# The last two chunks' down-projection of five feature pairs with seven block products for eight, columns by tokens

## The chip, the cores and the metric

The kernel runs on one core of a Trainium2 chip. The metric is the device time of one execution in microseconds (us). The core has five engines that run beside each other and wait for each other by semaphores: TensorE (PE, with its weight loads listed as PEld), VectorE (DVE), ScalarE (ACT), GpSimd (POOL) and SyncE (SP, which here only issues transfers). Matmuls read SBUF and write banks of PSUM (eight banks of 128 x 512 floats); DVE and ACT read and write both memories, POOL only SBUF.

## The reference

Strided attention on 8 x 8 heads gives 4608 tokens of 512 features, and two matrices follow, with the square of a ReLU between them:

```python
x = attn_out.transpose(0, 2, 1, 3).reshape(B * S, H * D)   # 4608 x 512
h = np.maximum(x @ w_in, 0.0)                              # w_in 512 x 2048
return (h * h @ w_out).astype(np.float32)                  # w_out 2048 x 512
```

Called here the up-projection (`x @ w_in`) and the down-projection (`h * h @ w_out`), in float32.

## The kernel before

**Precision.** A float32 matrix is kept as two fp32r tiles, high part and remainder, and each product is three matmuls: high by high, low by high, high by low. To split an operand, ACT casts the high part and another engine subtracts it (`features`, L720 and L721: ACT, then DVE).

**Tiling.** The tokens are nine chunks of 512 (`TC`), the 2048 features sixteen tiles of 128 (`NFT`), in eight pairs `p` of two (features 2p and 2p+1). `wi[p]` and `wo[p]` hold a pair's weights, as high and low. The up-projection (`up`, L738) gives a feature tile as 128 features x 512 tokens in one bank; ACT applies ReLU and square (`squared`, L725 and L726). The down-projection (`downs`, L772) uses 128 tokens of the squared tile as stationary operand and 512 columns of `w_out` as moving one: four banks of 128 tokens x 512 columns (`y_ps`) add up over the sixteen features, twelve matmuls a feature.

**The last two chunks.** Call them a (chunk 7) and b (chunk 8). Their pairs 0 to 2 (`MIX` = 3) go as above, and both chunks' up-projections of pairs 3 to 7 go together in `finale`, as 2 x 2 blocks by Winograd's form of Strassen's scheme: seven products (`product`, L994, six matmuls each) for eight. It needs differences of weights, made per pair by `combos` (L972 to L987 on POOL, ten instructions of 128 x 256, then L967 on ACT and L968 on DVE, four times each), and differences of the chunks' activations (`ts`, made once). Between the seven products of a pair, four groups of six matmuls of chunk a's down-projection of the pair before fill PE's queue (`fill`). Then come chunk a's last two features, and last, with nothing of other engines left to do but copying out, the whole of b's down-projection: 16 features, 192 matmuls. The last two features of a and of b are ordered by bank, so that banks are copied and stored while PE goes on.

**Order.** Each engine executes its queue in order. PE's order is that of the program (`pe` puts each group behind the one before, by `tc.issue_after`). On DVE, ACT and POOL a planner that schedules on simulated times takes what is ready, earlier program lines first. A tile of a pool waits until the buffer that it takes over is free, and the first tiles of a pool that is opened where another was closed wait for the last use of that other. Stores are issued on SP's queue, and the very last half bank on ACT's.

Of the kernel before, what the change touches and what calls it, by code (L numbers as in the profile page):

```python
# [83 lines left out]
def attn_moe(ctx: ExitStack, tc, qk_d, v_d, qk_p, v_p, kv_s, q_s, k_s, v_s, w_in, w_out, masks, consts, out):  # L84
# [674 lines left out]

    def downs(c, js):  # L760
# [21 lines left out]
        if end:  # L782
            for t in range(NTT):
                y = ypool.tile([P, DM], F32, name=f"ysb{c}_{t}", tag="ysb")
                dst = out[c * TC + t * P : c * TC + (t + 1) * P, :]
                if tail and t == NTT - 1:
                    m = DM // 2
                    for i, queue in ((0, nc.sync), (m, nc.scalar)):
                        nc.scalar.copy(y[:, i : i + m], y_ps[c][t][:, i : i + m])
                        queue.dma_start(out=dst[:, i : i + m], in_=y[:, i : i + m])  # L790
                else:
                    (nc.scalar.copy if t % 2 else nc.vector.tensor_copy)(y, y_ps[c][t])
                    nc.sync.dma_start(out=dst, in_=y)
            yield done
# [120 lines left out]

    def second(p):
# [4 lines left out]
        g = home(p)  # L921
        for i in range(2):
            features(b, 2 * p + i, held[b, 2 * p + i], (g[:, i, 0], g[:, i, 1]))

    def differences():
# [3 lines left out]
        late = pool("late", 1)  # L929
# [22 lines left out]
    def finale():  # L952
# [48 lines left out]
        second(MIX - 1)  # L1001
        turn = [0, 1, 4]
        for p in range(MIX, NFT // 2):
            fill = downs(a, [2 * p - 2, 2 * p - 1])
# [10 lines left out]
            squared(ba)  # L1015
            features(a, 2 * p, ba)
            last_one = p == NFT // 2 - 1
            for _ in range(1 if last_one else 2):
                pe(lambda: next(fill))
# [4 lines left out]
            squared(c22)  # L1024
            for _ in range(1 if last_one else 2):
                pe(lambda: next(fill))
            s_next = combos(p + 1) if p + 1 < NFT // 2 else None
# [6 lines left out]
            squared(bb)
            squared(u2)
            features(a, 2 * p + 1, u2)
            g = home(p)
            for i, src in enumerate((bb, c22)):
                features(b, 2 * p + i, src, (g[:, i, 0], g[:, i, 1]))
            s = s_next  # L1040
        pe(lambda: down(a, [NFT - 2, NFT - 1]))
        for j in range(0, NFT, 2):
            pe(lambda: down(b, [j, j + 1]))
# [105 lines left out]
```

## Time and profile before

| | before |
|---|---|
| median of 3 runs (lowest to highest) | 836.65 us (836.48 to 837.39) |
| profiled execution, its own time | 836.61 us |
| its span, first to last instruction | 834.6 us |
| PE busy | 825.1 us, 99% |
| DVE, POOL, ACT busy | 552.6, 578.2, 344.9 us |
| matmuls | 5973 |

The span is what lies between the first and the last instruction that the profiler saw; 2.0 us of the profiled execution's time lie around it. A row of the timeline gives start, duration, engine, line, operation and the tiles (out<-in) with their shape, and in brackets the idle time ahead of it and what ended that. Matmuls overlap in their records (each lasts 390 ns, and the next starts earlier), so the pace is read from start to start.

### The profile page before, as it was taken

The page shows a single profiled execution, that of the slowest core. Times are in us where ns is not written, and L with a number is a line of the kernel's source. Part 1 is how long each engine was busy: PE and PEld are TensorE (multiplying, and loading weights), DVE is VectorE, ACT ScalarE, POOL GpSimd, SP SyncE. Part 2 cuts the span into 40 slices and gives each one's busy share as a digit, 9 for nine tenths or more (in the row PEclk, how much of TensorE's full clock was granted, in tenths as well). Part 3 has the DMA queues.
Part 4 walks back from the last instruction along what each step waited for, and adds up shares of the span by engine and source line. Part 5 has one row for each costly group of instructions (what it writes and reads, how often), then busy time and mean ns, then how long its engine had stood idle before and what let it go on. Part 6 is the DMA issues. An engine that isn't in the chain of part 4 may idle for free.

```text
span 834.6 us, 14916 instructions
## 1 busy us (share of the span) xinstructions
PE 825.1 (99%) x5973; PEld 677.4 (81%) x5977; DVE 552.6 (66%) x997; ACT 344.9 (41%) x610; POOL 578.2 (69%) x594
## 2 busy tenths in 40 slices
PE   8999999999999999999999999999999999999998
PEld 5788888888888888888888888888888877888886
DVE  6979866785778567775688477866887884444200
ACT  5987743333333234333333333323333256556300
POOL 4597779786996878786978599697879387640000
PEclk9999999999999999999999999999999999999999
DMA  9974350113310431042113130033023000000101
GB/s 354 394 258 138 123 200 34 58 61 122 107 57 3 153 132 59 1 156 102 39 59 119 44 130 26 13 124 118 0 80 108 28 25 0 1 1 1 50 1 51
DMA packets 23653, 73.68 MB, mean 88 GB/s; under 512 B 2592, under 2 KB 6048, under 8 KB 21920
## 3 DMA queue, kind: packets, MB, share of 16 engines
q1 hardware_dynamic: 23296, 72.49, 24.9%
q8 instruction: 47, 0.77, 0.4%
q10 hardware_dynamic: 288, 0.24, 0.1%
q14 instruction: 22, 0.18, 0.1%
HBM read 63.28 MB, written 9.44 MB: 87 GB/s over the span
## 4 chain that ended last, share of the span: by engine, by line
PE 82%; DVE 6%; POOL 6%; issue 2%; DMA 2%; ACT 2%; SPq 0%; DVEq 0%; POOLq 0%
PE y L772 40%; PE h L738 33%; PE c L994 6%; POOL pp L545 3%; PE o L296 2%; POOL pq L545 2%; DVE pt L248 1%; DMA v<-v_d 1%; PE s L281 1%; DVE os L546 1%; DVE gl L721 1%; DVE b L940 1%; ACT h L725 0%; DVE b L937 0%; ACT gh L720 0%
## 5 line engine op out<-in xcount | busy, mean ns | idle before, releaser
L772 PE MATMUL y<-w,gh 128*128 128x512 f32 x1024 | 314.6, 390 | 0.0
L545 POOL TENSOR_TENSOR pq<-ks,qs 128x512 f32<-128x512 f32 (+7 forms) x184 | 208.4, 1160 | 49.5 <-DVE sc L546 45.3
L545 POOL TENSOR_TENSOR pp<-vs,sc 128x320 f32<-128x320 f32 (+11 forms) x184 | 201.1, 1121 | 53.8 <-DVE os L546 51.2
L772 PEld LDWEIGHTS y<-w,gh 128*128 128x128 f32 x1024 | 191.7, 188 | 40.1 <-POOL w L166 0.3
L772 PE MATMUL y<-w,gl 128*128 128x512 f32 x512 | 197.8, 389 | 0.0
L725 ACT ACTIVATE h<-h 128x512 f32<-128x512 f32 x120 | 69.9, 583 | 271.9 <-PE h L738 270.9
L546 DVE TENSOR_REDUCE sc<-pq 128x5 f32<-128x320 f32 (+6 forms) x192 | 113.0, 598 | 48.1 <-POOL pq L545 46.4
L546 DVE TENSOR_REDUCE os<-pp 128x32 f32<-128x384 f32 (+15 forms) x184 | 108.8, 602 | 51.2 <-POOL pp L545 49.8
L738 PE MATMUL h<-xlh,w 128*128 128x512 f32 x496 | 135.0, 393 | 1.5 <-DVE gb L721 1.4
L738 PE MATMUL h<-xsh,w 128*128 128x512 f32 x496 | 133.1, 389 | 0.0
L721 DVE TENSOR_TENSOR gl<-h,gh 128x512 fp32r<-128x512 f32 x118 | 80.5, 683 | 64.0 <-ACT gh L720 63.8
L772 PEld LDWEIGHTS y<-w,gl 128*128 128x128 f32 x512 | 96.1, 188 | 20.0
L738 PEld LDWEIGHTS h<-xlh,w 128*128 128x128 f32 x496 | 91.9, 188 | 22.3 <-DVE gb L721 2.7
L738 PEld LDWEIGHTS h<-xsh,w 128*128 128x128 f32 x496 | 93.1, 188 | 19.5
L738 PE MATMUL h<-xll,w 128*128 128x512 f32 x248 | 76.8, 390 | 0.0
L738 PE MATMUL h<-xsl,w 128*128 128x512 f32 x248 | 76.8, 389 | 0.0
L726 ACT ACTIVATE h<-h 128x512 f32<-128x512 f32 x120 | 69.9, 582 | 3.5
L720 ACT CAST gh<-h 128x512 fp32r<-128x512 f32 x118 | 69.4, 588 | 4.1 <-DVE h L749 0.9
L166 POOL TENSOR_TENSOR w<-raw,w 128x512 fp32r<-128x512 f32 x32 | 45.6, 1430 | 19.5 <-DVE w L162 10.5
L248 DVE STREAM_TRANSPOSE pt<-e 32x256 f32<-32x256 f32 x128 | 55.7, 435 | 2.3
L738 PEld LDWEIGHTS h<-xsl,w 128*128 128x128 f32 x248 | 46.5, 188 | 9.9 <-DVE xsl L502 0.2
L738 PEld LDWEIGHTS h<-xll,w 128*128 128x128 f32 x248 | 46.5, 188 | 9.8
(164 smaller groups left out, 784.9 us busy)
## 6 DMA issues: line engine op xcount, KB each, us to landing
vs<-v_s SPq DMA_DIRECT2D x18, 576.0 KB, 3.7
v<-v_d SPq DMA_DIRECT2D x18, 512.0 KB, 4.9
y<-ysb SPq DMA_DIRECT2D x35, 256.0 KB, 2.7
raw<-w_out SPq DMA_DIRECT2D x7, 1024.0 KB, 6.3
raw<-w_in SPq DMA_DIRECT2D x6, 1024.0 KB, 7.2
ks<-k_s SPq DMA_DIRECT2D x8, 576.0 KB, 3.8
qk<-qk_d SPq DMA_DIRECT2D x8, 560.0 KB, 4.8
qk<-qk_d SPq DMA_DIRECT2D x8, 544.0 KB, 5.0
```

Of the source, the lines that this page charges most:

```text
L166: last["g"] = nc.gpsimd.tensor_sub(lo, f32(w), f32(hi))
L248: nc.vector.transpose(out=pt[to : to + STR, :, STR * b : STR * (b + 1)], in_=e5[STR * b : STR * (b + 1), :, a, STR * half : STR * (half + 1)],
L296: last["mm"] = nc.tensor.matmul(o[a][D * h : D * (h + 1), at : at + STR], v5[pr][ks, h, w, b], pt[ks, (2 * h + pr) * 2 + w, STR * b : STR ...
L545: nc.gpsimd.tensor_mul(pv, x, y)
L546: nc.vector.tensor_reduce(out=to, in_=pv, op=ALU.add, axis=AX.X)
L720: last["gh"] = nc.scalar.copy(gh, ph)
L721: last["gl"] = lows[c, j] = nc.vector.tensor_sub(gl, ph, f32(gh))
L725: nc.scalar.activation(ph, ph, AF.Relu)
L726: nc.scalar.activation(ph, ph, AF.Square)
L738: done = nc.tensor.matmul(ph, wi[p][a][:, wsl], x["ls"[k // 2], b][:, k % 2, :], start=n == 0, stop=n == 11)
L772: done = nc.tensor.matmul(y_ps[c][t], gg[:, sl], w[:, wsl], start=j == 0 and k == 0, stop=j == NFT - 1 and k == 2)
L994: done = nc.tensor.matmul(bank, w[m][:, k], x[n][:, k], start=start and k == m == n == 0, stop=True, skip_group_check=True)
```

## The change

Pairs 3 to 7 of the down-projection of a and b get the same seven-for-eight scheme. The output is turned: stationary operand 128 columns of `w_out`, moving operand 512 tokens, so that a bank holds 128 columns x 512 tokens (`turned_down`, also for all features of chunk a and for b's pairs 0 to 2), and the host swaps the axes back in `unpack`. The blocks are two halves of the 512 columns, the pair's two features, and the two chunks; one product of one pair is six matmuls, three into each of two banks (`block`).

In the loop over pairs the four groups of filling matmuls a pair become one (`fill_first`, the product of the plain blocks, of the pair before), and the squared activations are kept whole in `gf` tiles, three of the four after a subtraction. After the loop pool `late` is closed and pool `tail` opened; then PE runs `fill_first` of pair 7, b's direct products into `W`, and six products one after another, each over all five pairs (`t3`, `b21`, `t2`, `t1`, `t4`, `b22`), and last b's direct products into `Y`. Each of the six needs its moving operand split for each pair (`operand`: ACT cast, DVE subtraction, 128 x 512), `t2` and `t4` also a subtraction ahead of that, and `t3`, `t2`, `t1` and `b22` sums of weights (`third`, `firsts`, `fourth`, of 128 x 256, on POOL or DVE).

The lines that the new loop replaces stand in the kernel above.

```diff
@@ -753,6 +753,13 @@
         features(c, j, ph)
         yield done
+    def turned_down(bank, p, o, t, g, start):
+        at = slice(o * DM + t * P, o * DM + (t + 1) * P)
+        for k, (m, n) in enumerate(((0, 0), (1, 0), (0, 1))):
+            done = nc.tensor.matmul(bank, wo[p][m][:, at], g[n], start=start and k == 0, stop=True, skip_group_check=True)
+        return done
     def down(c, js):
         *_, done = downs(c, js)
         return done
@@ -763,18 +770,16 @@
             y_ps[c] = [ybank(f"y{c}_{t}") for t in range(NTT)]
         g = [g_tiles.pop((c, j)) for j in js]
         end = js[-1] == NFT - 1
-        tail = end and c == NCHUNK - 1
         def part(t, j, gh, gl):
             p, o = divmod(j, 2)
             wsl, sl = slice(o * DM, (o + 1) * DM), slice(t * P, (t + 1) * P)
+            if c == NCHUNK - 2:
+                return turned_down(y_ps[c][t], p, o, t, (gh, gl), j == 0)
             for k, (gg, w) in enumerate(((gh, wo[p][0]), (gh, wo[p][1]), (gl, wo[p][0]))):
                 done = nc.tensor.matmul(y_ps[c][t], gg[:, sl], w[:, wsl], start=j == 0 and k == 0, stop=j == NFT - 1 and k == 2)
             return done
         steps = [(t, n) for n in range(len(js)) for t in range(NTT)]
-        if end and c >= NCHUNK - 2:
-            steps.sort()
         for m, (t, n) in enumerate(steps):
             done = part(t, js[n], *g[n])
             if m % 2:
@@ -783,14 +788,8 @@
...
-                if tail and t == NTT - 1:
-                    m = DM // 2
-                    for i, queue in ((0, nc.sync), (m, nc.scalar)):
-                        nc.scalar.copy(y[:, i : i + m], y_ps[c][t][:, i : i + m])
-                        queue.dma_start(out=dst[:, i : i + m], in_=y[:, i : i + m])
-                else:
...
+                (nc.scalar.copy if t % 2 else nc.vector.tensor_copy)(y, y_ps[c][t])
+                nc.sync.dma_start(out=dst, in_=y)
...
+    of_late = ctx.enter_context(ExitStack())
...
-        late = pool("late", 1)
+        late = of_late.enter_context(tc.tile_pool(name="late", bufs=1))
...
@@ -999,48 +1002,212 @@
         with tc.issue_after(last["sum"].ins):
             s = combos(MIX)
         second(MIX - 1)
+        NP = NFT // 2
+        g, fs = {}, {}
+        def up_sums(p):
+            fs[p] = combos(p)
+        fs[MIX] = s
+        direct_fill = downs(a, [2 * MIX - 2, 2 * MIX - 1])
+        def take_direct(n):
+            for _ in range(n):
+                pe(lambda: next(direct_fill))
+        def first_product(p, bank):
+            pe(lambda: product(bank, direct(p, 0, 0), x11, True))
+        def split_to(hi, lo, src, sub=nc.vector):
+            nc.scalar.copy(hi, src)
+            sub.tensor_sub(lo, src, f32(hi))
+        def block(banks, w, op, start, ts=range(2)):
+            for t in ts:
+                for k, (m, n) in enumerate(((0, 0), (1, 0), (0, 1))):
+                    done = nc.tensor.matmul(banks[t], w[m][:, t * P : (t + 1) * P], op[n], start=start and k == 0, stop=True, skip_group_check=True)
+            return done
+        def w_block(p, o, m):
+            return [t[:, o * DM + m * 256 : o * DM + (m + 1) * 256] for t in wo[p]]
+        b11 = {}
+        def fill_first(p):
+            pe(lambda: block(X, w_block(p, 0, 0), b11[p], p == MIX))
         turn = [0, 1, 4]
...
+        ba = psum(turn[0], f"c11_{MIX}")
+        first_product(MIX, ba)
+        for p in range(MIX, NP):
             na, nb, spare = turn
             turn = [spare, na, nb]
...
+            last_one = p == NP - 1
+            bb, bc = psum(nb, f"c12_{p}"), psum(3, f"c21_{p}")
+            nc.scalar.copy(bb, ba)
+            s = fs.pop(p)
+            if p > MIX:
+                fill_first(p - 1)
             pe(lambda: product(bc, s[3], ts[3], True))
...
             pe(lambda: product(bb, s[2], ts[2], False))
             u2 = ypool.tile([P, TC], F32, name=f"u2_{p}", tag="ysb")
             nc.scalar.copy(u2, bb)
...
+            pe(lambda: product(ba, direct(p, 1, 0), x21, False))
+            if p == MIX:
+                take_direct(2)
             pe(lambda: product(bb, s[1], ts[1], False))
             c22 = ypool.tile([P, TC], F32, name=f"c22_{p}", tag="ysb")
             nc.vector.tensor_copy(c22, bb)
+            squared(ba)
+            b11[p] = [gpool.tile([P, TC], F32R, name=f"b11{t}_{p}", tag=f"g{t}") for t in "hl"]
+            split_to(*b11[p], ba)
+            if p == MIX:
+                take_direct(2)
+                ds = [gpool.tile([P, TC], F32, name=f"d{t}", tag=("gh", "gl")[t % 2]) for t in range(4)]
+                for t in range(4):
+                    (nc.vector.tensor_copy if t % 2 else nc.scalar.copy)(ds[t], y_ps[a][t])
+                X, W = ([ybank(f"{nm}{t}") for t in range(2)] for nm in "xw")
             nc.vector.tensor_add(c22, c22, bc)
...
+            if not last_one:
+                ba_next = psum(spare, f"c11_{p + 1}")
+                first_product(p + 1, ba_next)
+                up_sums(p + 1)
+            else:
+                pe(lambda: [turned_down(W[t], 0, 0, 2 + t, [gb[0][:, 0, k] for k in range(2)], True) for t in range(2)][-1])
             pe(lambda: product(bb, s[4], x22, False))
             pe(lambda: product(bc, direct(p, 1, 1), ts[4], False))
...
             nc.vector.tensor_add(u2, u2, bc)
...
+            h = g[p] = wpool.tile([P, 4, TC], F32, name=f"gf{p}", tag=f"w{HOME[order.index((p, 0))]}")
+            for i, src in ((1, bb), (3, c22), (2, u2)):
+                nc.scalar.activation(src, src, AF.Relu)
+                nc.scalar.activation(h[:, i], src, AF.Square)
+                if i == 1:
+                    nc.vector.tensor_sub(h[:, 0], h[:, 1], ba)
+            nc.vector.tensor_sub(h[:, 1], h[:, 3], h[:, 1])
+            if not last_one:
+                ba = ba_next
+        of_late.close()
+        tail = of_late.enter_context(tc.tile_pool(name="tail", bufs=1))
+        PS = range(MIX, NP)
+        sums = {n: {} for n in (1, 2, 3, 4)}
+        def part(nm, p):
+            return tail.tile([P, 256], F32, name=f"q{nm}_{p}", tag="sf", bufs=3)
+        def kept_sum(n, p, src, e):
+            t = sums[n][p] = tail.tile([P, 2, 256], F32R, name=f"v{n}_{p}", tag="sd", bufs=8)
+            nc.scalar.copy(t[:, 0], src)
+            e.tensor_sub(t[:, 1], src, f32(t[:, 0]))
+            return [t[:, 0], t[:, 1]]
+        low = {}
+        blocks = lambda p: {(m, o): [f32(t) for t in w_block(p, o, m)] for m in range(2) for o in range(2)}
+        def third(p, e):
+            w = blocks(p)
+            s3, u = part("3", p), part("u", p)
+            e.tensor_sub(s3, w[0, 0][0], w[1, 0][0])
+            e.tensor_sub(u, w[0, 0][1], w[1, 0][1])
+            e.tensor_add(s3, s3, u)
+            sums[3][p] = kept_sum(3, p, s3, e)
+        s2s = {}
+        def firsts(p, e):
+            w = blocks(p)
+            s1, u = part("1", p), part("w", p)
+            e.tensor_add(s1, w[1, 0][0], w[1, 1][0])
+            e.tensor_add(u, w[1, 0][1], w[1, 1][1])
+            e.tensor_add(s1, s1, u)
+            s2 = s2s[p] = tail.tile([P, 256], F32, name=f"q2_{p}", tag="s2", bufs=5)
+            e.tensor_sub(s2, s1, w[0, 0][0])
+            e.tensor_sub(s2, s2, w[0, 0][1])
+            sums[2][p] = kept_sum(2, p, s2, e)
+            to = sums[1][p] = w_block(p, 0, 1)
+            nc.scalar.copy(to[0], s1)
+            e.tensor_sub(to[1], s1, f32(to[0]))
+        def fourth(p, e):
+            w, s4 = blocks(p), part("4", p)
+            e.tensor_sub(s4, w[0, 1][0], s2s[p])
+            e.tensor_add(s4, s4, w[0, 1][1])
+            sums[4][p] = kept_sum(4, p, s4, e)
+        ops, tags = {}, ["xlh", "xll", "xsh", "xsl", None, "xlh", "xll", "xsh", "xsl", None, None, None]
+        def operand(nm, p, src, sub=nc.vector):
+            tag = tags.pop(0)
+            tags.append(tag)
+            t = ops[nm, p] = (xpool.tile([P, 2, TC], F32R, name=f"{nm}_{p}", tag=tag) if tag else tail.tile([P, 2, TC], F32R, name=f"{nm}_{p}", tag="op", bufs=4))
+            split_to(t[:, 0], t[:, 1], src, sub)
+        def product_of(banks, nm, w, start=False):
+            for p in PS:
+                pe(lambda: block(banks, w(p), [ops[nm, p][:, k] for k in range(2)], start and p == MIX))
+        def outs(t, m, y, queue=nc.sync):
+            r = (a + m) * TC + t * P
+            queue.dma_start(out=out[r : r + P, :], in_=y)
+        fill_first(NP - 1)
+        Y = [psum(turn[0], "ya"), psum(turn[1], "yb")]
+        Z = [psum(turn[2], "za"), psum(3, "zb")]
+        for t in range(2):
+            nc.scalar.copy(Y[t], X[t])
+        for j in range(1, 2 * MIX):
+            pe(lambda: [turned_down(W[t], *divmod(j, 2), 2 + t, g_tiles[b, j], False) for t in range(2)][-1])
+        for p in PS:
+            third(p, nc.vector if p - MIX > 2 else nc.gpsimd)
+            operand("t3", p, g[p][:, 1])
+        product_of(Z, "t3", lambda p: sums[3][p], True)
+        for p in PS:
+            operand("b21", p, g[p][:, 2])
+        product_of(X, "b21", lambda p: w_block(p, 1, 0))
+        c22 = [gpool.tile([P, TC], F32, name=f"c22{t}", tag=f"g{'hl'[t]}") for t in range(2)]
+        for t in range(2):
+            nc.scalar.copy(c22[t], W[t])
+            nc.vector.tensor_add(c22[t], c22[t], Z[t])
+        for t in range(2):
+            y = ypool.tile([P, TC], F32, name=f"y11_{t}", tag="ysb")
+            nc.vector.tensor_add(y, ds[t], X[t])
+            outs(t, 0, y)
+        for p in PS:
+            firsts(p, nc.gpsimd if (p - MIX) % 2 else nc.vector)
+            nc.vector.tensor_sub(g[p][:, 1], g[p][:, 3], g[p][:, 0])
+            operand("t2", p, g[p][:, 1])
+        product_of(Y, "t2", lambda p: sums[2][p])
+        for t in range(2):
+            nc.vector.tensor_add(ds[2 + t], ds[2 + t], Y[t])
+        for p in PS:
+            operand("t1", p, g[p][:, 0])
+            fourth(p, nc.gpsimd)
+        product_of(Y, "t1", lambda p: sums[1][p])
+        for t in range(2):
+            nc.vector.tensor_add(c22[t], c22[t], Y[t])
+            outs(2 + t, 1, c22[t])
+        for p in PS:
+            nc.vector.tensor_sub(g[p][:, 2], g[p][:, 2], g[p][:, 1])
+            operand("t4", p, g[p][:, 2])
+        product_of(Z, "t4", lambda p: w_block(p, 1, 1))
+        for t in range(2):
+            nc.vector.tensor_add(ds[2 + t], ds[2 + t], Z[t])
+            outs(2 + t, 0, ds[2 + t])
+        for p in PS:
+            operand("b22", p, g[p][:, 3])
+        product_of(Y, "b22", lambda p: sums[4][p])
+        for t in range(2):
+            for j in range(2 * MIX):
+                pe(lambda: turned_down(Y[t], *divmod(j, 2), t, g_tiles[b, j], False))
+            y = ypool.tile([P, TC], F32, name=f"y12_{t}", tag="ysb")
+            if t == 0:
+                nc.vector.tensor_copy(y, Y[t])
+                outs(t, 1, y)
+            else:
+                m = TC // 2
+                for i, queue in ((0, nc.sync), (m, nc.scalar)):
+                    nc.scalar.copy(y[:, i : i + m], Y[t][:, i : i + m])
+                    queue.dma_start(out=out[b * TC + P : b * TC + 2 * P, i : i + m], in_=y[:, i : i + m])
...
@@ -1125,6 +1292,8 @@
...
+    y = y.reshape(NCHUNK, TC, DM).copy()
+    y[-2:] = y[-2:].swapaxes(1, 2)
...
```

## Rows read from the trace of the kernel before

**Rows 1.** The page: span, and busy time of each engine

```profile
span 834.6 us, 14916 instructions
PE 825.1 (99%) x5973; PEld 677.4 (81%) x5977; DVE 552.6 (66%) x997; ACT 344.9 (41%) x610; POOL 578.2 (69%) x594
```

**Rows 2.** The chain that ended last, in order of time: start, duration, engine, line

```profile
719.04 8.16 PE c L994 x36
734.00 8.16 PE c L994 x36
...
787.17 43.87 PE y L772 x192
...
831.07 0.65 ACT ysb L789 x2
```

**Rows 3.** Stretches: length, busy time (count) of PE, PEld, DVE, ACT, POOL; granted clock; DMA

```profile
0.00:5.00 5.00, 3.19 (x93) 1.51 (x94) 0.27 (x1) 1.49 (x2) 3.00 (x7) 1.00 0.61 197
...
680.00:700.00 20.00, 18.75 (x81) 14.54 (x79) 15.40 (x18) 11.81 (x25) 18.90 (x21) 1.00 0.00 0
...
740.00:760.00 20.00, 20.00 (x90) 16.57 (x89) 9.27 (x15) 12.13 (x24) 4.75 (x6) 1.00 0.01 1
...
800.00:820.00 20.00, 20.00 (x90) 16.53 (x90) 0.00 (x0) 0.00 (x0) 0.00 (x0) 1.00 0.00 0
```

**Rows 4.** Timeline of DVE, both operands in SBUF (at 717.29 one in PSUM)

```profile
675.26 0.69 DVE L949 TENSOR_TENSOR t1l<-b,t1h 128x512 fp32r<-128x512 f32 x1
675.87 0.69 DVE L940 TENSOR_TENSOR b<-b,b 128x512 f32<-128x512 f32 x1
...
681.73 1.22 DVE L937 TENSOR_TENSOR b<-xsh,xsl 128x512 f32<-128x512 f32 x1
682.88 2.38 DVE L940 TENSOR_TENSOR b<-b,b 128x512 f32<-128x512 f32 x2
685.17 1.22 DVE L949 TENSOR_TENSOR t1l<-b,t1h 128x512 fp32r<-128x512 f32 x1
...
692.59 1.51 DVE L968 TENSOR_TENSOR s<-f,s 128x256 fp32r<-128x256 f32 x2 [1.06 <-ACT s L967]
...
716.96 0.42 DVE L968 TENSOR_TENSOR s<-f,s 128x256 fp32r<-128x256 f32 x1
717.29 0.68 DVE L1023 TENSOR_TENSOR c<-c,c 128x512 f32<-128x512 f32 x1
```

**Rows 5.** Timeline of POOL at the same times

```profile
681.21 1.20 POOL L972 TENSOR_TENSOR f<-w 128x256 f32<-128x256 f32 x1
682.37 1.19 POOL L973 TENSOR_TENSOR fu<-w 128x256 f32<-128x256 f32 x1
...
692.90 0.92 POOL L972 TENSOR_TENSOR f<-w 128x256 f32<-128x256 f32 x1
693.78 0.92 POOL L987 TENSOR_TENSOR f<-f,w 128x256 f32<-128x256 f32 x1
...
698.57 0.74 POOL L981 TENSOR_TENSOR f<-f,w 128x256 f32<-128x256 f32 x1
699.39 0.73 POOL L982 TENSOR_TENSOR f<-f,w 128x256 f32<-128x256 f32 x1
...
721.86 0.74 POOL L973 TENSOR_TENSOR fu<-w 128x256 f32<-128x256 f32 x1 [3.67 <-DVE s L968]
...
745.18 0.73 POOL L987 TENSOR_TENSOR f<-f,w 128x256 f32<-128x256 f32 x1
```

**Rows 6.** Timeline of DVE with one operand in PSUM

```profile
722.45 1.30 DVE L721 TENSOR_TENSOR gb<-c,gb 128x512 fp32r<-128x512 f32 x2
```

**Rows 7.** Groups of ACT lines from 680 us on: busy time, mean ns

```profile
L720 ACT CAST gb<-c 128x512 fp32r<-128x512 f32 x10 | 5.5, 602 | 0.4 <-PE c L994 0.4
L967 ACT CAST s<-f 128x256 fp32r<-128x256 f32 x20 | 8.1, 410 | 13.1 <-PE c L994 9.1 <-POOL f L982 3.2 <-POOL f L987 0.8
```

**Rows 8.** Timeline of PE where the loop over pairs begins

```profile
707.86 0.73 PE L994 MATMUL c<-t3h,s 128*128 128x512 f32 x2 [0.55 <-DVE gb L721]
```

More of the change, by code (lines that the diff above doesn't have):

```diff
@@ L785, in downs @@
                 dst = out[c * TC + t * P : c * TC + (t + 1) * P, :]
-                if tail and t == NTT - 1:
-                    m = DM // 2
-                    for i, queue in ((0, nc.sync), (m, nc.scalar)):
-                        nc.scalar.copy(y[:, i : i + m], y_ps[c][t][:, i : i + m])
-                        queue.dma_start(out=dst[:, i : i + m], in_=y[:, i : i + m])
-                else:
-                    (nc.scalar.copy if t % 2 else nc.vector.tensor_copy)(y, y_ps[c][t])
-                    nc.sync.dma_start(out=dst, in_=y)
+                (nc.scalar.copy if t % 2 else nc.vector.tensor_copy)(y, y_ps[c][t])
+                nc.sync.dma_start(out=dst, in_=y)
             yield done
@@ L914, in home @@
         return wpool.tile([P, 2, 2, TC], F32R, name=f"gb{p}", tag=f"w{HOME[order.index((p, 0))]}")
+    gb = {}
     def second(p):
@@ L920, in second @@
             pe(lambda: list(up(b, j, (3, 4)[j % 2]))[-1])
-        g = home(p)
+        g = gb[p] = home(p)
         for i in range(2):
             features(b, 2 * p + i, held[b, 2 * p + i], (g[:, i, 0], g[:, i, 1]))
+    of_late = ctx.enter_context(ExitStack())
     def differences():
@@ L1001, in finale @@
         second(MIX - 1)
+        NP = NFT // 2
[22 more added lines that the diff above has]
+            pe(lambda: block(X, w_block(p, 0, 0), b11[p], p == MIX))
         turn = [0, 1, 4]
-        for p in range(MIX, NFT // 2):
-            fill = downs(a, [2 * p - 2, 2 * p - 1])
+        ba = psum(turn[0], f"c11_{MIX}")
+        first_product(MIX, ba)
+        for p in range(MIX, NP):
             na, nb, spare = turn
             turn = [spare, na, nb]
-            ba, bb, bc = psum(na, f"c11_{p}"), psum(nb, f"c12_{p}"), psum(3, f"c21_{p}")
-            pe(lambda: product(ba, direct(p, 0, 0), x11, True))
+            last_one = p == NP - 1
[4 more added lines that the diff above has]
+                fill_first(p - 1)
             pe(lambda: product(bc, s[3], ts[3], True))
-            nc.scalar.copy(bb, ba)
-            pe(lambda: product(ba, direct(p, 1, 0), x21, False))
             pe(lambda: product(bb, s[2], ts[2], False))
@@ L1014, in finale @@
             nc.scalar.copy(u2, bb)
[L1015 to L1019, printed above, removed]
+            pe(lambda: product(ba, direct(p, 1, 0), x21, False))
+            if p == MIX:
+                take_direct(2)
             pe(lambda: product(bb, s[1], ts[1], False))
@@ L1022, in finale @@
             nc.vector.tensor_copy(c22, bb)
-            nc.vector.tensor_add(c22, c22, bc)
[L1024 to L1027, printed above, removed]
+            squared(ba)
[7 more added lines that the diff above has]
+                X, W = ([ybank(f"{nm}{t}") for t in range(2)] for nm in "xw")
@@ L1028, in finale @@
+            nc.vector.tensor_add(c22, c22, bc)
+            if not last_one:
[4 more added lines that the diff above has]
+                pe(lambda: [turned_down(W[t], 0, 0, 2 + t, [gb[0][:, 0, k] for k in range(2)], True) for t in range(2)][-1])
             pe(lambda: product(bb, s[4], x22, False))
             pe(lambda: product(bc, direct(p, 1, 1), ts[4], False))
-            if last_one:
-                for _ in range(2):
-                    pe(lambda: next(fill))
@@ L1033, in finale @@
             nc.vector.tensor_add(u2, u2, bc)
[L1034 to L1043, printed above, removed]
+            h = g[p] = wpool.tile([P, 4, TC], F32, name=f"gf{p}", tag=f"w{HOME[order.index((p, 0))]}")
```

## The prediction

> **What bounds the kernel now.** The page's busy times come first: PE is busy 825.1 of 834.6 us, every other engine 70% or less [rows 1]. The chain of waits ends in PE alone: blocks of 36 matmuls in the loop over pairs, then 192 in one piece, then two half copies and the last store [rows 2]. Two pairs start 14.96 us apart (734.00 - 719.04) with 42 + 24 = 66 matmuls each: 0.2267 us a matmul, back to back. In the stretches, POOL's work is over by 746 us [rows 5] and nobody but PE works from 800 to 820 us [rows 3]. So PE's count sets the time of the finale, and the other engines have some 40 us of room at the end. The change takes from the first and fills the second.
>
> **PE's side of the sum.** Before, the finale has 5 x 42 up, 5 x 24 fillers, 24 of chunk a's last features and 192 of b: 546 matmuls. After: 5 x 42 up; seven products of 30, the fillers among them, 210; direct ones 24 (a's pair 2) + 36 (`W`) + 36 (`Y`): 516. Instructions of the same shape, so 30 x 0.2267 = 6.8 us go. The end stays: 18 matmuls into the last bank, two half copies, a store of each half; nine stores before and nine after, SP's queue has room. The wait of 0.55 us at the loop's start [rows 8] stays too, since bank 3 is written second in either order.
>
> **The loop over pairs.** A pair shrinks from 66 matmuls to 48, 14.96 to 10.88 us. ACT's 512-wide operations go from 14 to 11 a pair and DVE's from 7 to 6 (the 256-wide ones of `combos` stay); POOL's ten stay, 1.2 each where DVE is always at work [rows 5], 12 us, and 8.2 us alone. The nearest new chain: the next pair's `bb` takes the bank of this pair's `ba`, which isn't free until ACT's square (0.60, after the pair's last product since it lands in the place of `wi[p]`), DVE's subtraction of `ba` (0.69) and ACT's copy (0.60) are through, about 2.1 us with the hand-overs, against 18 matmuls, 4.1 us. That hides it. Without cover it is 4 turns x 2.1. Bounds: 0, and 4 x (14.96 - 10.88) = 16 if POOL's pauses (3.67 us in one wait for DVE [rows 5]) don't shrink with the pair. POOL's waits follow products of PE, which come closer together as well, so I take 0.5.
>
> **The six products after the loop.** Call T0 the end of the loop's last product. PE then has 36 matmuls with nothing to wait for (8.2 us), and then six products of five blocks (1.36 us each). What they need, counted from the diff: ACT 30 casts of 512 and 20 of 256, 0.60 and 0.41 [rows 7], 26 us in 49: hidden. DVE 40 subtractions of 512 with both operands in SBUF (30 `operand`, 10 of `gf` tiles), 29 of 256 (`third` of two pairs 8, `firsts` of three pairs 21), and 11 of 512 with one in PSUM. POOL 41 of 256 (`third` 12, `firsts` 14, `fourth` 15).
>
> What these cost is the point. Alone, DVE does the 512 in 0.69 and the 256 in 0.42, POOL the 256 in 0.74 [rows 4, 5]; from start to start in a queue that is 0.61 to 0.62, 0.33 to 0.35 and 0.82 [rows 4, 5]. From 681 to 687 us both have work without a pause, all operands in SBUF: each DVE instruction of 512 lasts 1.15 to 1.22 us and each POOL instruction of 256 1.18 to 1.20, one beginning where the other ends, both once in 1.15 us. They take turns. Where DVE's are of 256 (two in 1.51 at 692.59), POOL's starts are 0.88 apart (692.90, 693.78). If a DVE instruction holds up POOL in proportion to its length, the difference gives 0.27 for 256 and 0.54 for 512, and POOL's own hold is 1.15 - 0.54 = 0.61. With an operand in PSUM, two DVE instructions take 1.30 while POOL works: not held up [rows 6]. So each POOL instruction can cost DVE 0.61.
>
> Take the last block of `t2`, 120 matmuls or 27.2 us after T0. By then DVE must have done: 20 of 512 (operands of `t3`, `b21`, `t2` and one row of subtractions), less four of `t3` that can run ahead of T0, 16 x 0.62 = 9.9; 29 of 256, 10.2; seven others of the loop's end and of the first sums' copying out, 7 x 0.66 = 4.6. Together 24.7 us: alone it just fits. POOL must have done 12 + 14 = 26, holding 26 x 0.61 = 15.9. If every hold falls on a waiting DVE instruction, DVE is through at 40.6, and PE has stood 13.4 us. If the two share without any loss, 15.9 + 16 x 0.54 + 29 x 0.27 = 32.4 us, begun 1.4 us ahead of T0 (pool `tail` waits for the last use of `late`, the product before the last): 31.0, PE stands 3.9. The rows of 681 to 687 show every hold landing on DVE, so I go near the upper end, less what the seven PSUM operations hide (4.6 us long, of which I take half): 11.0. The three scratch tiles (`sf`, two held by each `third` and `firsts`) push the same way. After `t2`, 90 matmuls (20.4 us) to the last block of `b22`, DVE has 20 x 0.62 + 6 x 0.66 = 16.4 and POOL holds 15 x 0.61 = 9.2: 25.6 with every hold, 9.2 + 20 x 0.54 = 20.0 shared; between 5.2 late and on time. Here `fourth` has two products' time to be made ahead, so I take 0, and leave 5.2 to the range. A wait of PE holds up everything behind it, as its order is fixed: no direct product stands between the six.
>
> **Sum**, against the profiled execution's 836.6 (median 836.65): - 6.8 + 0.5 + 11.0 = 841.3 us.
>
> **A rule that speaks further against it.** In the rows, PE's granted clock is 1.00 (2.4 GHz) in each stretch, also where PE is busy only 3.19 of 5 us or 18.75 of 20 [rows 3]; in my sum it would be busy about 7 of 18 us in `t2`, which no row shows. The Trainium skill, "TensorE: Matmul & The Clock Gate", Part 1, says that the clock is halved when PE has been idle and comes back after sustained work. By that rule blocks between the pauses would take twice as long. This is the third rival.
>
> **Rivals.** First, faster: the take-turns cost falls into time that DVE would have been idle, because the planner puts POOL's sums of weights ahead and DVE's free subtractions between. Then the lossless sharing decides, 2 to 4 us, 832.3 to 834.3. For it: `b21` and `t4` need no sums of weights, and DVE is busy only 9.27 of 20 us in the loop [rows 3]. Against: pool `tail` can't begin sooner, and 681 to 687 us show no such sharing when both are loaded. The point from which it decides: a stall under 4.6 us. Between the two (4.6 to 8 us of stall) nothing measurable remains, 835.0 to 838.3. Second, slower than forecast: scratch tiles hand over one by one. A `third` on POOL lasts 3 x 1.15 + 0.41 + 1.15 = 5.0, on DVE 4 x 0.88 + 0.41 = 3.9, a `firsts` 7 x 1.15 + 0.41 = 8.5 and 7 x 0.88 + 0.41 = 6.6; three, two, two and three of them make 15 + 8 + 17 + 20 = 60 us end to end; with one and a quarter at a time 48, less 1.4 and 27.2, a stall of 19: 849. For it: three tiles, two to a job. Against: the second tile is back after the third instruction. Third, PE falls to 1.2 GHz in the pauses: ten blocks after them (`t1`, `t4`) at twice 1.36 add up to 13.6, most of it under DVE's remaining work; with 6 of it, 847. For it: the long pauses of the sum. Against: 1.00 in every row. Fourth, the loop over pairs becomes POOL's: 12 us a pair against 10.88, 4 x 1.1 = 4.5 more; it is in the range. That the products are not saved can't be: the count is in the program.
>
> **Chances.** Forecast 0.42 (838.5 to 845), faster 0.30, no difference 0.12, the second rival 0.11, the third 0.05. A difference under 0.2% (1.7 us) can't be told from none here. So faster 0.30, same 0.12, slower 0.58. With both signs in play the range runs from 831 (lossless sharing) to 850 (second rival); the forecast's own is 838.5 to 845.
>
> **What would show it.** Right: 516 of these matmuls at 0.2267 us; PE idle ahead of blocks of `t3` and above all of `t2`, released by DVE or POOL sums of weights; DVE's 512-wide subtractions at 1.1 to 1.3 us while POOL works, 0.7 after; no PE gap over 0.5 us at a pair's turn; a filled stretch of 36 matmuls at the end. Wrong: PE back to back from T0 on; DVE's subtractions at 0.7 us beside a busy POOL; gaps in the loop; waits on ACT; a granted clock under 1.

## The result, and the profile after

The changed kernel takes 848.4 us (847.37 to 849.03), the kernel before 836.83: a ratio of 1.0136, 95% interval [1.0119, 1.0154]. It is slower by 11.6 us; forecast were 4.7. The profiled execution takes 849.03 us, against 836.61.

The page of the changed kernel answers to [rows 1]: PE's busy time rises although the program has 30 matmuls less (26 by the two pages, since a few records can be missing from a trace).

```profile
span 847.2 us, 15032 instructions
PE 827.5 (98%) x5947; PEld 674.2 (80%) x5947; DVE 602.7 (71%) x1070; ACT 361.3 (43%) x648; POOL 616.3 (73%) x635
```

The chain that ended last, in order of time, shows the loop over pairs, as [rows 2] did: 10.88 us from one pair to the next, as forecast.

```profile
724.72 9.52 PE c L997 x42
735.60 9.52 PE c L997 x42
```

The timeline of PE shows what follows the loop. The first row answers to [rows 8]; the bracket is the idle time before a row and what ended it.

```profile
708.10 0.73 PE L997 MATMUL c<-t3h,s 128*128 128x512 f32 x2 [0.55 <-DVE gb L721]
...
768.62 6.96 PE L760 MATMUL w<-gb,w 128*128 128x512 f32 x30
...
782.30 0.50 PE L1028 MATMUL za<-t,v 128*128 128x512 f32 x1 [1.33 <-ACT v L1100]
...
784.67 1.07 PE L1028 MATMUL za<-t,v 128*128 128x512 f32 x2 [1.64 <-DVE v L1101]
...
788.73 6.96 PE L1028 MATMUL x<-b,w 128*128 128x512 f32 x30
...
800.87 0.50 PE L1028 MATMUL ya<-t,v 128*128 128x512 f32 x1 [2.08 <-ACT v L1100]
...
805.36 1.22 PE L1028 MATMUL ya<-t,v 128*128 128x512 f32 x2 [3.76 <-DVE v L1101]
...
810.56 0.50 PE L1028 MATMUL ya<-t,v 128*128 128x512 f32 x1 [1.07 <-ACT v L1100]
...
812.13 1.21 PE L1028 MATMUL ya<-t,v 128*128 128x512 f32 x2 [0.83 <-DVE v L1101]
...
814.12 1.63 PE L1028 MATMUL ya<-t,w 128*128 128x512 f32 x3
...
835.32 4.24 PE L760 MATMUL ya<-gb,w 128*128 128x512 f32 x18
839.40 4.24 PE L760 MATMUL yb<-gb,w 128*128 128x512 f32 x18
```

The loop's last product ends at 767.26. From there 252 matmuls at 0.2267 us would be 57.1 us; the last ends at 843.64, 76.4 us later. The 19.3 us between fall thus (stage starts read from the timeline):

| stage | from, to | at 0.2267 us | lost |
|---|---|---|---|
| 36 with nothing to wait for | 767.26, 775.42 | 8.2 | 0 |
| `t3`, 30 | 775.42, 788.73 | 6.8 | 6.5 |
| `b21`, 30 | 788.73, 795.53 | 6.8 | 0 |
| `t2`, 30 | 795.53, 814.12 | 6.8 | 11.8 |
| `t1`, `t4`, `b22`, 90 | 814.12, 835.32 | 20.4 | 0.8 |
| direct, 36 | 835.32, 843.64 | 8.2 | 0.1 |

So `t3` and `t2`, the first two products whose weights are sums, lose 18.3 of the 19.3 us. VectorE (with ScalarE's copy between) releases nearly every block. The stretches, as in [rows 3], show VectorE with almost no pause there, and mostly idle after it; the column behind POOL's is the granted clock:

```profile
780.00:785.00 5.00, 2.02 (x7) 1.07 (x7) 5.00 (x11) 1.62 (x4) 0.00 (x0) 0.99 0.00 0
785.00:790.00 5.00, 5.00 (x16) 3.60 (x16) 4.88 (x11) 1.95 (x4) 2.25 (x3) 0.67 0.01 2
...
800.00:805.00 5.00, 0.73 (x2) 0.30 (x2) 5.00 (x8) 1.85 (x4) 5.00 (x6) 0.69 0.28 105
805.00:810.00 5.00, 4.13 (x10) 2.99 (x10) 5.00 (x8) 1.44 (x3) 3.19 (x5) 0.62 0.00 0
...
820.00:825.00 5.00, 5.00 (x24) 4.14 (x23) 1.91 (x3) 0.00 (x0) 0.00 (x0) 1.00 0.28 105
```

Two matmuls at 805.36 take 1.22 us, at full clock 0.62 to 0.73. The granted clock was 1.00 in [rows 3]; here a stretch's mean lies between its two levels, 2.4 and 1.2 GHz, after TensorE has stood.

What VectorE did meanwhile is in its groups of lines from 767 to 812 us (mean ns of one). GpSimd's timeline answers to [rows 5], and VectorE's shows `t2`'s last sum:

```profile
L1023 DVE TENSOR_TENSOR t<-gf,t 128x512 fp32r<-128x512 f32 x16 | 14.1, 882 | 0.1
...
L1190 DVE TENSOR_TENSOR gf<-gf 128x512 f32<-128x512 f32 x5 | 5.5, 1095 | 0.0
```

```profile
765.71 1.21 POOL L1110 TENSOR_TENSOR q<-w 128x256 f32<-128x256 f32 x1 [22.89 <-DVE c L1070]
...
787.31 1.26 POOL L1120 TENSOR_TENSOR q<-w 128x256 f32<-128x256 f32 x1 [7.59 <-DVE v L1101]
```

```profile
811.13 0.94 DVE L1101 TENSOR_TENSOR v<-q,v 128x256 fp32r<-128x256 f32 x1
```

L1190 is a row of subtractions that `t4` needs, which starts at 821.72. Of the sixteen `t` of L1023, one is of `t3` and five are of `t2`; ten are of `t1` and `t4`, all of theirs. With one of `b22` (0.97 us at 810.23) that is 5.5 + 10 x 0.88 + 1.0 = 15.3 us of VectorE's time, ahead of the end of `t2`'s last sum (812.07), for products that come later. In return, five of the subtractions that `t3`, `b21` and `t2` need were done, or begun, ahead of the loop's end at 767.26, beside four of `t3` (VectorE's timeline: the row of subtractions for `t2`, four of five, and the first of `b21`):

```profile
754.96 1.28 DVE L1177 TENSOR_TENSOR gf<-gf 128x512 f32<-128x512 f32 x2
...
762.63 0.69 DVE L1177 TENSOR_TENSOR gf<-gf 128x512 f32<-128x512 f32 x1
...
765.63 0.69 DVE L1177 TENSOR_TENSOR gf<-gf 128x512 f32<-128x512 f32 x1
766.24 1.23 DVE L1023 TENSOR_TENSOR b<-gf,b 128x512 fp32r<-128x512 f32 x1
```

### The profile page after: what moved, and what is told of

It is laid out like the page before. It is cut to its first block, busy times and chain, and to the rows that moved or that the text cites. A ratio compares the mean times of both kernels' runs of the same rounds, so it can differ in the third digit from the quotient of the medians.

```text
span 847.2 us, 15032 instructions
## 1 busy us (share of the span) xinstructions
PE 827.5 (98%) x5947; PEld 674.2 (80%) x5947; DVE 602.7 (71%) x1070; ACT 361.3 (43%) x648; POOL 616.3 (73%) x635
## 4 chain that ended last, share of the span: by engine, by line
PE 85%; DVE 6%; DMA 4%; ACT 2%; POOL 1%; issue 1%; SPq 0%; DVEq 0%; ACTq 0%
PE h L738 36%; PE y L779 35%; PE c L997 5%; PE o L296 2%; PE s L281 1%; DMA kv<-kv_s 1%; PE ya L1028 1%; DVE t L1023 1%; DMA v<-v_d 1%; PE yb L1028 1%; DMA raw<-w_out 1%; DVE b L943 1%; PE x L1028 1%; PE y L760 1%; DVE b L1023 1%
## 5 line engine op out<-in xcount | busy, mean ns | idle before, releaser
L779 PE MATMUL y<-w,gh 128*128 128x512 f32 x896 | 276.0, 390 | 0.2 <-POOL w L166 0.2
L779 PEld LDWEIGHTS y<-w,gh 128*128 128x128 f32 x896 | 167.6, 188 | 35.6 <-POOL w L166 0.6
L779 PE MATMUL y<-w,gl 128*128 128x512 f32 x448 | 173.4, 389 | 0.0
L779 PEld LDWEIGHTS y<-w,gl 128*128 128x128 f32 x448 | 84.1, 188 | 17.5
```

## The experiments

Three causes were open: GpSimd's reads hold up VectorE (A); VectorE does work ahead of its time (B); the scratch tiles are handed over one by one (C). And what part has the clock?

**GpSimd only writes.** For A.

```diff
+        class writes_only:
+            tensor_add = tensor_sub = staticmethod(lambda to, x, y: nc.gpsimd.memset(f32(to), 0.5))
...
-            third(p, nc.vector if p - MIX > 2 else nc.gpsimd)
+            third(p, nc.vector if p - MIX > 2 else writes_only)
```

(and so in `firsts` and `fourth`)

> Changed kernel, but POOL's 41 instructions for the sums of weights only write (each fills its tile with a constant; the sums that POOL made are left out of the computation). Same tiles, same waits for them, but POOL reads nothing from SBUF. Theory 'turns' (a POOL instruction that reads SBUF holds up a DVE instruction with two SBUF operands for 0.61 us): DVE's 512-wide subtractions fall back to about 0.68 us and the 256-wide to 0.41 while POOL works, and some 11 of PE's 19 us of standing go: about 837 us. Theory 'order' alone (DVE does work that isn't due yet ahead of work that is): DVE's queue is as full of it as before, 845 us or more.

Measured 833.35 us, ratio to before 0.9962 [0.9949, 0.9975]: 15.0 us less than the changed kernel, and 3.7 below what the turns were expected to give. But a write lasts 0.312 us, and so GpSimd's sums came sooner as well. The next kernel takes that away.

**Four writes for one**, GpSimd as slow as it was.

```diff
-lambda to, x, y: nc.gpsimd.memset(f32(to), 0.5)
+lambda to, x, y: [nc.gpsimd.memset(f32(to), 0.5) for _ in range(4)][-1]
```

> As the kernel in which GpSimd's 41 instructions only write (833.35 us, its sums left out), but each write done four times over: 4 x 0.312 = 1.25 us, so that GpSimd is as slow as it was in the changed kernel (1.07 to 1.21 an instruction) and no longer reads. Theory (its hold on VectorE is what costs 15 us): VectorE keeps 0.69 and 0.42; GpSimd's first three sums take 15 us from 766, so that the third block of t3 stands some 3 us; 834 to 838. Rival (TensorE waited for GpSimd's late sums, not for VectorE): 845 to 849.

Measured 835.55 us, 0.9985 [0.9976, 0.9994], as expected of the holds. One stretch of 75 us, 765 to 840, in the same columns as above, of the changed kernel, of the single writes and of the fourfold ones:

```profile
765.00:840.00 75.00, 63.33 (x246) 48.15 (x245) 54.39 (x78) 27.00 (x56) 39.62 (x41) 0.91 0.06 22
```

```profile
765.00:840.00 75.00, 60.88 (x261) 48.16 (x259) 39.73 (x78) 27.38 (x58) 10.91 (x40) 0.99 0.08 29
```

```profile
765.00:840.00 75.00, 62.27 (x265) 48.70 (x264) 41.05 (x79) 28.16 (x58) 41.43 (x160) 0.98 0.08 29
```

Read the third and the fifth pair: GpSimd is busy 39.62 us with reads, and VectorE takes 54.39 us for 78 instructions; GpSimd is busy 41.43 us with writes alone, and VectorE takes 41.05 for 79. The group of `t` with the fourfold writes says the same, 688 ns for 882:

```profile
L1023 DVE TENSOR_TENSOR t<-gf,t 128x512 fp32r<-128x512 f32 x16 | 10.8, 688 | 0.8 <-ACT t L1022 0.8
```

GpSimd's slowness costs 835.55 - 833.35 = 2.2 us, its reads 848.4 - 835.55 = 12.9 (a write also waits for no input of a sum, which these two kernels don't separate from the reads; VectorE's shorter instructions don't hang on that). A is shown. The Trainium skill, "SBUF — State Buffer", section "SBUF: two separate sides", has the rule: a VectorE instruction with two SBUF inputs and a GpSimd instruction that reads SBUF exclude each other through a port that they share, and one that only writes is not concerned. These rows agree with it.

**All sums on VectorE.**

```diff
-            third(p, nc.vector if p - MIX > 2 else nc.gpsimd)
+            third(p, nc.vector)
...
-            firsts(p, nc.gpsimd if (p - MIX) % 2 else nc.vector)
+            firsts(p, nc.vector)
...
-            fourth(p, nc.gpsimd)
+            fourth(p, nc.vector)
```

> Changed kernel with all sums of weights on DVE (third, firsts and fourth for each pair), POOL idle after the loop. DVE gets 41 more instructions of 256, 14 us at 0.35. 'Turns': the holds are worth more than that, so PE's standing falls from 19 to about 11 us and the time to 838 to 841 us. If the holds cost little and DVE is simply overloaded: 14 us more, 858 to 862 us.

Measured 844.96 us, 1.0100 [1.0085, 1.0115], between the two cases expected. The same stretch:

```profile
765.00:840.00 75.00, 65.26 (x261) 49.14 (x259) 53.02 (x118) 27.99 (x58) 0.00 (x0) 0.95 0.07 25
```

VectorE does all 118 instructions in 53.02 us; with GpSimd's help it needed 54.39 for 78. The 41 sums cost it 14.0 us to do (53.02 - 39.73, and 0.7 because one other instruction falls outside this stretch), and 14.7 (54.39 - 39.73) to have done. But 8 us over the kernel before remain, so A is not all.

**VectorE's later work put behind the last sum of `t2`**, alone. For B.

```diff
+            if p == NP - 1:
+                due.append(last["sub"])
...
-            operand("t1", p, g[p][:, 0])
+            with behind_due():
+                operand("t1", p, g[p][:, 0])
```

(and so for the subtractions of `t4` and `b22`)

> Changed kernel, with DVE's subtractions for the products t1, t4 and b22 put behind the last DVE instruction that t2 waits for (an ordering edge on DVE's own queue, no other wait). 'Order' (16 instructions of 512 that aren't due stand ahead of those that are, by 812 us): PE's standing ahead of t2 shrinks by 5 to 8 us, 841 to 844 us. 'Turns' alone, with DVE never short of due work: no change ahead of t3, little ahead of t2, 847 to 849 us.

Measured 849.43 us, 1.0152 [1.0137, 1.0167]: no gain, where order was expected to give 841 to 844. `t2` is through at some 802.7 for 814.1; then PE stands 10.49 us (PE's timeline, then VectorE's):

```profile
813.23 1.65 PE L1028 MATMUL ya<-t,w 128*128 128x512 f32 x3 [10.49 <-DVE d L1187]
```

```profile
801.16 5.76 DVE L1023 TENSOR_TENSOR t<-gf,t 128x512 fp32r<-128x512 f32 x5
806.84 5.74 DVE L1198 TENSOR_TENSOR gf<-gf 128x512 f32<-128x512 f32 x5
812.50 0.68 DVE L1187 TENSOR_TENSOR d<-d,ya 128x512 f32<-128x512 f32 x1
```

The additions that free the Y banks (L1187) stand behind ten subtractions of 1.15 us. The run doesn't speak against B: `t2` did come some 11 us sooner, and one late piece of work was put for another. A kernel further down mends it.

**More scratch tiles**, for C: five of `sf` for three, seven of `sd` for eight.

> Changed kernel with five scratch tiles for the sums of weights for three (and seven for eight of the tiles that keep a sum, for the space). Theory 'scratch' (third and firsts hold two tiles each, so that POOL stood still 7.6 us and DVE's two thirds came late): POOL's pause of 7.6 us goes, PE's standing ahead of t3 falls from 6.5 to about 2 us, and the time by 5 to 8 us, 841 to 843 us. 'Turns' or 'order' alone: the tiles were not what was waited for, 847 to 849 us.

Measured 849.78 us, 1.0155 [1.0138, 1.0172], no gain. GpSimd's pause of 7.59 us is down to 2.97 (GpSimd's timeline), but PE's longest waits stay, elsewhere:

```profile
782.62 6.34 POOL L1120 TENSOR_TENSOR q<-w 128x256 f32<-128x256 f32 x1 [2.97 <-DVE q L1112]
```

```profile
785.01 1.22 PE L1028 MATMUL za<-t,v 128*128 128x512 f32 x2 [2.58 <-DVE v L1101]
...
805.95 1.22 PE L1028 MATMUL ya<-t,v 128*128 128x512 f32 x2 [5.56 <-DVE v L1101]
```

With the sums on VectorE the tiles make it no better:

> All sums of weights on VectorE (844.96 us alone) and five scratch tiles for three, seven of the kept sums for eight (849.78 us alone, a loss of 1.4). Theory that the scratch tiles don't matter (VectorE's own queue is full and nobody else uses them): 844 to 846. Rival (with one engine the hand-over of a scratch tile from ScalarE's copy back to VectorE is what stops it, and five take that away): 841 or less.

Measured 845.77 us, 1.0102 [1.0087, 1.0118], as expected where the tiles don't matter. C falls.

**Only the later of the late work put off**: as in the kernel of 849.43 us, but `t1`'s subtractions stay where they were, and those of `t4` and `b22` go behind the additions.

```diff
-            nc.vector.tensor_add(ds[2 + t], ds[2 + t], Y[t])
+            added = nc.vector.tensor_add(ds[2 + t], ds[2 + t], Y[t])
...
-            nc.vector.tensor_sub(g[p][:, 2], g[p][:, 2], g[p][:, 1])
-            operand("t4", p, g[p][:, 2])
+            with tc.issue_after(added.ins):
+                nc.vector.tensor_sub(g[p][:, 2], g[p][:, 2], g[p][:, 1])
+                operand("t4", p, g[p][:, 2])
...
-            operand("b22", p, g[p][:, 3])
+            with tc.issue_after(added.ins):
+                operand("b22", p, g[p][:, 3])
```

> Changed kernel with VectorE's subtractions for t4 and b22 queued behind the two additions of the Y banks to ds, those of t1 where they were: so the additions, which stood behind late work in the run with the order alone, stand behind nothing. Theory (VectorE did 11 instructions before their time, some 11 us at 0.9 to 1.1 each beside GpSimd, and TensorE stood for them): t2 is through at 804 to 807 for 814.1; some 3 us come back at t4, whose ten subtractions now have 8 us: 841 to 845. Rival (what leaves one stage comes back whole in the next, as in the run with the order alone): 847 to 850.

Measured 842.62 us, 1.0067 [1.0052, 1.0083], in the middle of what was expected: 5.8 us gained by order alone. `t1` starts at 807.40 for 814.12, and one wait comes back at `t4`:

```profile
767.86 0.62 PE L1028 MATMUL x<-b11h,w 128*128 128x512 f32 x2
...
807.40 0.97 PE L1028 MATMUL ya<-t,w 128*128 128x512 f32 x3 [0.32 <-DVE d L1181]
...
816.73 0.50 PE L1028 MATMUL za<-t,w 128*128 128x512 f32 x1 [1.32 <-DVE t L1023]
```

```profile
804.28 0.43 DVE L1101 TENSOR_TENSOR v<-q,v 128x256 fp32r<-128x256 f32 x1 [0.47 <-ACT v L1100]
```

B is shown. The last row is VectorE's end of `t2`'s sums, and the first is the loop's end: 126 matmuls lie between it and 807.40, 28.6 us at 0.2267, so PE has stood 39.5 - 28.6 = 11.0 us by the end of `t2`, where the changed kernel stood 18.3.

**PE's pauses filled with matmuls that nobody reads.** Do the pauses hold other work, and what does the clock cost?

```diff
+        direct_y = [(t, j) for t in range(2) for j in range(2 * MIX)]
...
-        def product_of(banks, nm, w, start=False):
+        def product_of(banks, nm, w, start=False, among=0):
             for p in PS:
+                for t, j in [direct_y.pop(0) for _ in range(among)] if p > MIX else ():
+                    pe(lambda: turned_down(W[t], *divmod(j, 2), t, g_tiles[b, j], j == 0))
...
-        product_of(Y, "t2", lambda p: sums[2][p])
+        product_of(Y, "t2", lambda p: sums[2][p], among=3)
```

> Changed kernel (848.4 us) plus 36 matmuls that nobody reads: a second time the direct products of b12, into the two W banks, nine ahead of each of blocks 2 to 5 of t2. They are 36 x 0.227 = 8.2 us of TensorE more. Theory (TensorE stands in t2 for 11.8 us because of VectorE and GpSimd, and some of what is lost besides is the halved clock that follows a pause): the 8.2 us lie wholly in the pauses, the granted clock stays near 1.0 in the stretches where it was 0.62 to 0.72, and the time is 846 to 849. Rival (it is TensorE's own instructions that release what VectorE waits for, scratch tiles or operands, so that a later block makes a later release): each matmul is paid, 848.4 + 8.2 = 856.6. In between (a pause at block 2 of only 2.08 us is filled, those of blocks 3 and 5 are unequal): 851.

Measured 850.43 us, 1.0157 [1.0143, 1.0170], near the case in between: 8.2 us of matmuls cost 2.0. Each nine take 2.2 us, and the granted clock, 0.69, 0.62 and 0.72 in the changed kernel's stretches from 800 to 815, is 1.00:

```profile
805.74 2.21 PE L760 MATMUL w<-gb,w 128*128 128x512 f32 x9
...
815.00 0.96 PE L1028 MATMUL ya<-t,w 128*128 128x512 f32 x3 [2.29 <-DVE d L1185]
```

```profile
800.00:805.00 5.00, 3.25 (x15) 2.40 (x14) 5.00 (x7) 1.58 (x4) 4.37 (x5) 1.00 0.28 105
805.00:810.00 5.00, 5.00 (x23) 4.11 (x22) 4.93 (x8) 1.95 (x5) 3.67 (x5) 1.00 0.01 3
810.00:815.00 5.00, 2.71 (x13) 1.90 (x12) 2.02 (x4) 1.33 (x3) 5.00 (x7) 1.00 0.00 0
```

The full clock didn't show in the time. `t2` is through at 812.7 for 814.1, but VectorE had taken up a subtraction for `b22` ahead of the additions of Y, and stood 2.98 us for ScalarE's cast of it, hence the 2.29 us (VectorE's timeline):

```profile
813.42 0.93 DVE L1023 TENSOR_TENSOR b<-gf,b 128x512 fp32r<-128x512 f32 x1 [2.98 <-ACT b L1022]
814.27 0.67 DVE L1185 TENSOR_TENSOR d<-d,ya 128x512 f32<-128x512 f32 x1
```

**The direct matmuls of `b12` in those pauses**, which now do useful work; the last ones no longer follow `b22`.

```diff
+        y12 = [ypool.tile([P, TC], F32, name=f"y12_{t}", tag="ysb") for t in range(2)]
+        for t in range(2):
+            nc.scalar.copy(y12[t], W[t])
         product_of(Y, "b22", lambda p: sums[4][p])
...
-                pe(lambda: turned_down(Y[t], *divmod(j, 2), t, g_tiles[b, j], False))
...
+                nc.vector.tensor_add(y[:, to], y[:, to], Y[t][:, to])
```

(with the edit of the kernel before it)

> Changed kernel with the 36 direct matmuls of b12, which it runs last of all, put into the W banks nine ahead of each of blocks 2 to 5 of t2; at the end ScalarE has copied these banks out and VectorE adds what the Y banks hold. Same arithmetic. Theory (TensorE has nothing to do there while VectorE is at work): 8.2 us of its work move into 11.8 us of standing: 848.4 - 8.2 = 840.2, less up to 2 us where the clock then stays at 1.0, plus some 0.5 us for an end with an addition instead of a copy: 838.5 to 841. Rival (TensorE's progress sets VectorE's): no gain, 848 to 849.

Measured 842.21 us, 1.0057 [1.0044, 1.0071]: 6.2 of the 8.2 us. The forecast missed by 1.2.

**Put together.** All sums on VectorE, five scratch tiles, the filling:

> All sums on VectorE, five scratch tiles, and the 36 direct matmuls of b12 in t2's pauses. If the two gains add (VectorE without GpSimd's holds 844.96 - 848.4 = -3.4; filling -8.2): 836.8, no better than the kernel before (836.7). If the standing left in t2 without the holds (about 3.5 us by its waits 1.07, 1.37 and 1.07) is less than the 8.2 us moved into it, TensorE becomes the bound there and the gain of the filling is 3.5 to 5: 840 to 841.5. If VectorE's full queue sets all of the standing after t2 as well, so that every microsecond moved ahead counts: 832 to 834, which beats the kernel before.

Measured 838.87 us, 1.0023 [1.0014, 1.0032], between the first two cases: the filling brings 845.77 - 838.87 = 6.9, much as before. VectorE still did `t4`'s subtractions and the fourth sums early. With those behind the additions of Y, as above:

> All sums on VectorE, five scratch tiles, 36 direct matmuls in t2's pauses (838.87 us so far), and VectorE's work for t4, b22 and the fourth sums behind the additions of Y to ds. By the profile of 838.87 VectorE executes five subtractions of 0.61 for t4 and fifteen of 0.34 us for the fourth sums before 811, some 8 us, and is idle after 815. Theory: these 8 us go from the 8.4 us for which TensorE stands in t3 and t2 and fit behind it: 832 to 835, faster than the kernel before. Rival (the fourth sums come too late for b22 and make a new wait): 838 or more.

Measured 834.76 us, 0.9982 [0.9973, 0.9990]: faster than both kernels, by 1.9 us and by 13.6. PE's timeline holds three waits, and the mean granted clock is 1.000:

```profile
780.51 0.72 PE L1028 MATMUL za<-t,v 128*128 128x512 f32 x2 [1.19 <-DVE v L1101]
...
793.23 0.73 PE L1028 MATMUL ya<-t,v 128*128 128x512 f32 x2 [1.53 <-DVE v L1101]
...
822.73 0.74 PE L1028 MATMUL ya<-b,v 128*128 128x512 f32 x2 [0.18 <-DVE v L1101]
```

And the same without the filling:

> The version of 834.76 us without its move of the 36 direct matmuls: all sums on VectorE, five scratch tiles, VectorE's work for t4, b22 and the fourth sums behind the additions of Y. There VectorE is done with t2's last sum at 799.9 and then stands 7.4 us, and TensorE takes up the 27 matmuls of three fills after the standing of 1.53 us at t2's second block. Theory that the filling is what hides VectorE's last sums of t2: these 27 x 0.227 = 6.1 us of cover go, VectorE's last sums come at 800 to 801 for a last block that could start at 795, some 4 to 5 us of standing, less some 2 us that the end gains by its older form and by a t4 that is ready sooner: 836.5 to 839. Rival (with the order right VectorE alone is fast enough, and the fill is not needed): 834 to 835.

Measured 836.18 us, 0.9997 [0.9988, 1.0006], just under what was expected. By its waits PE stands some 1.6 us more, not 4 to 5:

```profile
779.43 0.74 PE L1028 MATMUL za<-t,v 128*128 128x512 f32 x2 [1.18 <-DVE v L1101]
...
792.14 0.73 PE L1028 MATMUL ya<-t,v 128*128 128x512 f32 x2 [1.50 <-DVE v L1101]
...
795.35 0.73 PE L1028 MATMUL ya<-t,v 128*128 128x512 f32 x2 [1.37 <-DVE v L1101]
```

So with the engine and the order right, filling is worth only some 1.4 us; in the changed kernel it was worth 6.2 because there was so much to fill.

## Why the prediction was right and wrong

- **PE's side, -6.8, right.** 252 matmuls follow the loop, back to back where nothing is awaited (36 in 8.16 us). The end stayed as long: 847.2 - 843.64 = 3.6 us, before 834.6 - 831.04 = 3.6 [rows 1, 2].
- **The loop, 0.5, right.** 10.88 us a pair and no wait over 0.2 us at a turn; the 0.55 of [rows 8] stayed. From the row with that wait to the loop's end it takes 0.7 us more than at 0.2267 us a matmul (59.16 for 258), and the kernel before 0.4 up to 787.17 (79.31 for 348): 0.2 more. GpSimd didn't become its bound (fourth rival).
- **The six products, 11.0, is the term that failed:** 19.3 measured, and 848.4 lies above the forecast's own 838.5 to 845. By the terms, - 6.8 + 0.2 + 19.3 = 12.7, and 849.03 - 836.61 = 12.4. The place was right (`t3` and `t2`, released by sums of weights), and so was the mechanism of the turns. What failed is the step "By then DVE must have done": it counted only what was due, 24.7 us. VectorE's queue also held 16 subtractions for `t1`, `t4` and `b22`, taken up as soon as their inputs were there. On the other side, five of the 16 that I counted as due were done ahead of the loop's end or begun there. So the list was 11 instructions too short, 6.8 us at their own 0.62. VectorE was through with `t2` at 812.07, 44.8 us after the loop's end, beyond the 40.6 of my upper bound and 6.6 beyond the 27.2 + 11.0 that I took: the list accounts for that. The halved clock in the blocks that follow, 1.1 and 0.8, makes up about the rest of the 8.3 us.
- **The run with the order alone bears that out.** With the work for `t4` and `b22` put off (842.62 us), VectorE has 16 such subtractions after the loop's end, as many as I counted (11 that are due and five of `t1`). It is through with `t2` at 804.71, 36.9 us after the loop's end, where my sum has 38.2, and PE stands 11.0 us up to the end of `t2`, as I took. That the two agree to the tenth is luck, since the 11.0 hold some of the halved clock (two matmuls in 1.22 us at 803.58), which my sum has not.
- **VectorE's holds were right in sum, and in part by luck.** Of the 44.8 us, 44.8 - 24.7 - 6.8 = 13.3 are left for it, and I took 38.2 - 24.7 = 13.5. But I counted 26 GpSimd instructions, 0.52 us each; 33 fall into that time (eight of them for `fourth`, which was not due either), at 0.40 each. Over the whole stretch it is 14.7 / 41 = 0.36. The 0.61 was a bound, as I called it.
- **After `t2`, 0, right:** 0.8 us, and that by the clock. What VectorE did too early it no longer had to do.
- **First rival (free subtractions between): half of it happened**, with the opposite sign. They did come between, and ahead of what was awaited.
- **Second rival (scratch tiles, 849)** named nearly the time that came, by chance: its mechanism is one that the runs refute, 849.78 with five tiles.
- **Third rival (halved clock):** it did occur, 0.62 to 0.72 in the stretches. The Trainium skill, "TensorE: Matmul & The Clock Gate", Part 1, has it so: the clock is halved when TensorE has been idle. By the timeline the blocks at 784.67, 805.36, 812.13 and 814.12 take 1.8, 1.7, 1.1 and 0.8 us more than at full clock, 5.4 us of the 19.3. It is a surcharge on the pauses, not a case of its own: the 1.7 lie ahead of a block that had to wait anyhow. What it cost net was not isolated, since the run that held the clock up brought another wait.

## What to carry to other kernels

Count on a busy engine not only what a stage needs but everything whose inputs are ready by then: its queue does that too, and what is early for a later product is late for this one. An elementwise helper on GpSimd is no help to a saturated VectorE if both read SBUF: 41 instructions taken over cost VectorE 14.7 us, doing them itself 14.0. Where the engine's order is mended, put off only what is not next, or the wait moves to the next product, as it did for 10.49 us.

## What the runs showed that was not expected

A pause doesn't by its own length decide on the clock. After a wait of 1.64 us in `t3` two matmuls took 1.07 us in the changed kernel (784.67); at the same place, after a wait of the same 1.64, they took 0.73 in the kernel with the matmuls that nobody reads (PE's timeline):

```profile
784.25 0.73 PE L1028 MATMUL za<-t,v 128*128 128x512 f32 x2 [1.64 <-DVE v L1101]
```

And the turns aren't always even: with five scratch tiles the GpSimd instruction at 782.62, shown above, lasted 6.34 us. While it did, VectorE executed eleven instructions at their own 0.41 and 0.68 us, one after another, and GpSimd's was over 0.6 us after VectorE paused (788.37). What decides on the turn was not tested.
